# First sequence of an attention and channel-mix kernel by halves of its heads, with its second scores turned round, a ScalarE share in the weight conversion, and gates begun with the first heads

## The chip, the cores and the metric

One core of a Trainium2 chip. The metric is device time in microseconds for one execution, the median of three runs. Engines are named as in the profile: PE is TensorE, DVE is VectorE, ACT is ScalarE, POOL is GpSimd, SP is SyncE, which here only issues loads and stores.

## The reference

```python
B, H, S, D = 8, 8, 576, 64;  NP = 32;  DM, DF = 512, 1024
def sm_attn(qq, kk, vv):
    s = scale * qq @ kk.T;  a = exp(s - max(s))
    return (a / (sum(a) + 1e-9)) @ vv
packed = sm_attn(p, k, v)            # 32 packed rows a head
out    = sm_attn(q, packed, packed)  # 576 tokens a head
x  = out, heads side by side         # (8, 576, 512)
xp = x, shifted by one token
xk = mu_k * x + (1 - mu_k) * xp;  xr = mu_r * x + (1 - mu_r) * xp
return sigmoid(xr @ w_r) * (relu(xk @ w_k) ** 2 @ w_v)
```

The activations are fp32, the three weight matrices arrive as 64-bit floats.

## The kernel before

The 4608 tokens are cut into nine blocks of 512. For every block PE multiplies gates (`w_r`, 48 products), keys (`w_k`, 96) and values (`w_v`, 96); each product is 512 columns wide. An fp32 product is three products of fp32r parts, high by high, high by low and low by high. This makes 2160 wide products (`gates`, L976 to L978; `keys`, L936 to L938; values, L1005 to L1007).

The weights are converted on the chip: `convert` takes a piece of 128x512, makes an fp32 pattern out of the two 32-bit halves of each number (ACT L309, DVE L311, L313, L315) and splits it into high (ACT L319) and low (DVE L321). There are 20 pieces: `w_r` 4, `w_k` 8, `w_v` 8.

The attention of a sequence has these steps: keys and queries are loaded (`raw`) and transposed on PE against `ident` (L415, queries of the first sequence L455); p is made block-diagonal with a stream transpose (`pt`, L482); first scores (L503); maximum, exponential (L585, L592); the softmax weights transposed (L606, L607); their product with the values (L532); the packed rows transposed (L553); second scores with the packed rows on partitions (L667 for the first sequence, L687 for others); a stream transpose on DVE, the softmax over 32 entries, and a stream transpose back (L703 and on). For later sequences x is then multiplied (L746) and mixed with its shifted copy on ACT and DVE (L897, L901). For the first one the shares mu and 1-mu are multiplied into the packed rows (`shared`, L783, L791), and PE makes xr and xk of the first block right out of the softmax weights `a2t` (`mixed_on_pe`, L806), by halves of the tokens (`hf`).

The order of the work is not written by hand. `Flow` runs all these parts as generators; each step names its engine and an estimated time, and the planner takes the step that can start first, ties and near ones by a rank (`RANK_...`, `FIRST`). The result is one fixed list for each engine. Where it sees PE waiting, ahead of `keep_busy`, it writes fill products (`spare`, L1085), 128x128 against `ident`, whose result nobody reads. `gates` of the first block ends that time. All loads are issued by `load` (L227), on SP's queue. In the time of the first loads the planner has ACT and DVE shared between attention and conversion.

Of the kernel before, what the change touches and what calls it, by code (L numbers as in the profile page):

```python
# [182 lines left out]
def attn_pack_channel_mix(ctx: ExitStack, tc: tile.TileContext, q, k, v, p, mu_k, mu_r, w_k, w_v, w_r, out):  # L183
    nc = tc.nc
# [21 lines left out]
    FIRST = 9.944, 10.165, 11.85, 12.0  # L206
    RANK_1, RANK_MIX, RANK_KEYS, RANK_R, RANK_W, RANK_W2, RANK_V, LOADS_1, RANK_SQ, RANK_REST, HOLD_V, HOLD_S = 12.793, 9.086, 9.325, 12.0, 13.15, 14.582, 15.08, 14.446, 12.17, 12.101, 0.1, 0.1
# [17 lines left out]
    def load(dst, src, issue, us):  # L225
        yield "queue", issue, None, None
        nc.sync.dma_start(dst, src)  # L227
        begin = max(flow.free.get("dma", 0.0), flow.t + 0.46)
        flow.free["dma"] = begin + us
        flow.free["queue"] = max(flow.free["queue"], begin - 2.0)  # L230
        flow.now.t = begin + us + LANDS
# [58 lines left out]

    def convert(w, hi, lo, c, o, n, event, first=None):
# [15 lines left out]

        yield act(n)
        nc.scalar.activation(m.bitcast(F32), w1.bitcast(F32), AF.Copy, scale=2.0 ** -112)  # L309
        yield vec2(n)  # L310
        nc.vector.tensor_scalar(m, m, 3, None, op0=ALU.logical_shift_left)  # L311
        yield vec(n, after=0.0)
        nc.vector.scalar_tensor_tensor(m, w1, 0x80000000, m, op0=ALU.bitwise_and, op1=ALU.bitwise_or)  # L313
        yield vec(n, after=0.0)
        nc.vector.scalar_tensor_tensor(m, w0, 29, m, op0=ALU.logical_shift_right, op1=ALU.bitwise_or)  # L315
# [17 lines left out]

    def loads(b):
        flow.spawn(packed(b), lrank(b) - (0.03 if b else 0.015))
        for src, tag in ((k, "kT"), (v, "vt"), (q, "qT")):
# [5 lines left out]
            if b == 0 and tag == "qT":  # L342
                yield from first_queries()
                continue
            for pr in range(NPR):

                space = "xk" if b == 0 else "raw"
# [24 lines left out]
    def back_to_issue():  # L372
        flow.now.t = flow.free["queue"]

    def values_of(b, h):

        slot = yield from flow.take("vt")
        vt = tile_([P, NPR, 5 * D], F32, "vt", slot)
        if b < MOVED:
            yield from load(  # L380
                vt[:, :, :4 * D], v[b, h::2, :NQ, :].rearrange("h (p c) d -> p h (c d)", c=4), 0.46, 1.8
            )
            back_to_issue()
            yield from load(vt[:S - NQ, :, 4 * D:], v[b, h::2, NQ:, :].rearrange("h p d -> p h d"), 0.63, 0.45)
# [20 lines left out]
    def transposed_on_pe(tag, b, pr, raw_space, raw_slot, raw):  # L405
# [11 lines left out]
        yield act(S)  # L417
        nc.scalar.copy(t.rearrange("p (a b) -> p a b", a=2), pT[:, :, :HS])
# [3 lines left out]

    def first_queries():

        raws = []
        for pr in range(NPR):
            space = "xk" if pr == NPR - 1 else "raw"
            slot = yield from flow.take(space)
            raws.append((space, slot, tile_([P, 6, 2 * D], F32, space, slot, "raw")))
        for pr, (space, slot, raw) in enumerate(raws):  # L430
            for hh in range(2):
                yield from load(
                    raw[:T6, :, hh * D:(hh + 1) * D], q[0, 2 * pr + hh].rearrange("(c p) d -> p c d", p=T6), 0.51, 0.6,
                )
                back_to_issue()
            for hf in range(2):
                flow.spawn(
                    first_transposed(pr, hf, space, slot, raw), rank(0) + (0.02 if hf else 0.0), flow.free["dma"] + LANDS
                )

    def first_transposed(pr, hf, raw_space, raw_slot, raw):
# [16 lines left out]
        if pr % 2:  # L458
# [8 lines left out]
    def packed(b):  # L467
# [16 lines left out]
        flow.set(("pt", b))  # L484

# [8 lines left out]
    def front(b):  # L494
# [23 lines left out]
        together = b > 0  # L518
        if together:
            yield from flow.wait(*((tag, b, h) for tag in ("aT", "vt") for h in range(2)))  # L520
            yield pe(1.4)
        for h in range(2):
            if not together:
                yield from flow.wait(("aT", b, h), ("vt", b, h))
                yield pe(0.65)
# [33 lines left out]
        first = None  # L559
        if b == 0:  # L560
            sx = yield from flow.take("xt")

            a2 = tile_([P, 2, S + 1], F32, "xt", sx, "a2t")
            nc.gpsimd.memset(a2[:, :, 0:1], 0.0)
            first = dict(a2=(sx, a2), left=4)
            flow.spawn(shared(ppT, first), RANK_MIX - 0.1)
            for hf in range(2):
                flow.spawn(half_scores(hf, sp, pm, ppT, left, first), rank(b, hf) - 1)
            return
# [89 lines left out]
    def half_scores(hf, sp, pm, ppT, left, first):  # L659

        yield from flow.wait(*(("qT", 0, pr, hf) for pr in range(NPR)))
        slot = yield from flow.take("pa")
        yield pe(0.7)
        s2 = banks(slot)
        for pr in range(NPR):
            for h, own in enumerate(HALVES):
                nc.tensor.matmul(  # L667
                    s2[32 * pr:32 * pr + 32, h, :HS], ppT[own, 32 * pr:32 * pr + 32],
                    ts["qT", 0, pr][1][own, hf * HS:(hf + 1) * HS],
                    start=True, stop=True,  # L670
                )
        flow.set(("s2", 0, hf))
        if ("s2", 0, 1 - hf) in flow.when:
            for pr in range(NPR):
                flow.give("kq", ts.pop(("qT", 0, pr))[0])
        yield from back(0, hf, sp, pm, slot, s2, left, first)

    def scores(b, sp, pm, ppT, left):
# [16 lines left out]
        for hf in range(2):  # L695
            flow.spawn(back(b, hf, sp, pm, slots[hf], s2[hf], left, None), rank(b, hf) - 1)

    def back(b, hf, sp, pm, slot, s2, left, first):
# [8 lines left out]
        m2 = sb.tile([P, NTB], F32, name="m2", tag=f"m2{hf}")  # L707
# [15 lines left out]
        if first:  # L723
            yield vec(S)
            nc.vector.transpose(
                first["a2"][1][:, :, 1 + hf * HS:1 + (hf + 1) * HS].rearrange("p h (k b) -> p h k b", b=32),
                e.rearrange("p (h k) b -> p h k b", h=2),
            )
            flow.give("e", se)
            for j, res, tag in ((2, xrs, "xr"), (0, xks, "xk")):  # L730
                flow.spawn(mixed_on_pe(hf, j, res, tag, first), RANK_MIX if tag == "xr" else RANK_KEYS)
            if hf:
                flow.spawn(rest_of_first(sp, pm, first), RANK_REST)
            return
# [42 lines left out]
    def shared(ppT, first):  # L777

        yield from flow.wait("mu")
        st = yield from flow.take("sig")  # L780
        ppTs = tile_([P, 4, NPR, NP], F32, "sig", st, "ppTs")
        yield vec(4 * P)
        nc.vector.tensor_tensor(  # L783
# [330 lines left out]
```

## Time and profile before

| | us |
|---|---|
| median of three runs | 597.06 (596.43 to 598.03) |
| profiled execution, its span from first to last instruction | 594.0 |
| PE busy in it | 584.2 |
| DVE / ACT busy | 370.9 / 309.2 |
| first gate product / first key product begins | 37.67 / 57.53 |

The profiled execution shows its span alone; the 3.06 us to the median are what lies around it and the spread. A busy PE counts fill products too. An instruction of fp32 operands leaves two records on PE, so that 24 records of `spare` are 12 instructions. Starts of successive records are a better measure of a product than its duration, since records overlap.

### The profile page before, as it was taken

To read this page: it belongs to the slowest core of one execution; us is meant where nothing else is said; L and a number is where in the kernel's file an instruction comes from. 1 tells how busy PE (TensorE), PEld (TensorE's weight loads), DVE (VectorE), ACT (ScalarE), POOL (GpSimd) and SP (SyncE) were. 2 spreads that over 40 slices of the span, in tenths; PEclk is the share of its full clock that TensorE was granted. 3 is DMA by queue.
4 is the path that set the end of the run, shared out by engine and by line. 5 is a ranking of instruction groups with operands and counts; after the bars stand their busy time and mean duration, and the time that the engine had idled before them with its cause. 6 is when DMAs were issued, how large, how long until landed. Compare 5 with 4: busy or idle time off the path is not lost.

```text
span 594.0 us, 10276 instructions
## 1 busy us (share of the span) xinstructions
PE 584.2 (98%) x3965; PEld 458.9 (77%) x3965; DVE 370.9 (62%) x721; ACT 309.2 (52%) x548; POOL 2.1 (0%) x22
## 2 busy tenths in 40 slices
PE   9999999999999999999999999999999999999997
PEld 8776767787778777777777787777788888888885
DVE  2698999956692788867874698269314712641321
ACT  3557884644663458468537392548425613721410
POOL 0000000000000000000000000000000000000000
PEclk9999999999999999999999999999999999999999
DMA  8988460764727076486076375200100010001001
GB/s 214 266 207 258 164 139 17 162 173 73 150 46 189 12 154 143 129 143 141 3 195 135 65 140 134 58 1 1 72 1 1 1 72 0 1 0 72 0 1 71
DMA packets 164095, 56.51 MB, mean 95 GB/s; under 512 B 141000, under 2 KB 155344, under 8 KB 164048
## 3 DMA queue, kind: packets, MB, share of 16 engines
q1 hardware_dynamic: 164048, 55.87, 39.3%
q8 instruction: 31, 0.51, 0.4%
q14 instruction: 16, 0.13, 0.1%
HBM read 42.86 MB, written 12.98 MB: 94 GB/s over the span
## 4 chain that ended last, share of the span: by engine, by line
PE 80%; DVE 13%; SPq 3%; DMA 1%; issue 1%; ACT 1%; DVEq 0%
PE ph L936 10%; PE pvo L1005 10%; PE ph L937 10%; PE ph L938 10%; PE pvo L1007 10%; PE pvo L1006 10%; PE pr L976 5%; PE pr L977 5%; PE pr L978 5%; SPq L227 3%; DVE m L313 2%; DVE m L315 2%; PE pa L532 2%; PE pa L746 2%; PE pa L687 1%
## 5 line engine op out<-in xcount | busy, mean ns | idle before, releaser
L936 PE MATMUL ph<-xk,wk_h 128*128 128x512 f32 x288 | 114.8, 399 | 0.0
L1005 PE MATMUL pvo<-wv_h,sq 128*128 128x512 f32 x288 | 113.8, 395 | 0.0
L937 PE MATMUL ph<-xk,wk_h 128*128 128x512 f32 x288 | 112.5, 391 | 0.0
L938 PE MATMUL ph<-xk,wk_l 128*128 128x512 f32 x288 | 112.3, 390 | 0.0
L1006 PE MATMUL pvo<-wv_l,sq 128*128 128x512 f32 x288 | 112.2, 389 | 0.0
L1007 PE MATMUL pvo<-wv_h,sq 128*128 128x512 f32 x288 | 112.1, 389 | 0.0
L954 DVE CAST sq<-r 128x512 fp32r<-128x512 f32 x72 | 30.0, 416 | 122.0 <-ACT r L950 119.4
L947 ACT ACTIVATE r<-ph 128x512 f32<-128x512 f32 x72 | 43.0, 597 | 85.8 <-PE ph L938 85.5
L1005 PEld LDWEIGHTS pvo<-wv_h,sq 128*128 128x128 f32 x288 | 54.0, 188 | 16.5 <-issue 5.4
L936 PEld LDWEIGHTS ph<-xk,wk_h 128*128 128x128 f32 x288 | 54.1, 188 | 16.0 <-issue 4.1
L1007 PEld LDWEIGHTS pvo<-wv_h,sq 128*128 128x128 f32 x288 | 54.1, 188 | 11.4
L938 PEld LDWEIGHTS ph<-xk,wk_l 128*128 128x128 f32 x288 | 54.1, 188 | 11.4
L937 PEld LDWEIGHTS ph<-xk,wk_h 128*128 128x128 f32 x288 | 54.1, 188 | 11.0 <-DVE xk L843 0.6
L1006 PEld LDWEIGHTS pvo<-wv_l,sq 128*128 128x128 f32 x288 | 54.1, 188 | 10.7
L976 PE MATMUL pr<-wr_h,xr 128*128 128x512 f32 x144 | 57.5, 399 | 0.4 <-DVE sig L1016 0.3
L901 DVE SCALAR_TENSOR_TENSOR x<-xt,mus,x 128x64 f32<-128x64 f32 (+7 forms) x120 | 54.0, 495 | 6.0 <-ACT x L897 5.9
L977 PE MATMUL pr<-wr_l,xr 128*128 128x512 f32 x144 | 56.2, 390 | 0.0
L978 PE MATMUL pr<-wr_h,xr 128*128 128x512 f32 x144 | 56.1, 390 | 0.0
L897 ACT ACTIVATE x<-xt,mus 128x64 f32<-128x64 f32 (+7 forms) x120 | 54.4, 514 | 0.1
L987 ACT ACTIVATE sig<-pr 128x512 f32<-128x512 f32 x36 | 21.4, 601 | 60.7 <-PE pr L978 47.4
L956 DVE TENSOR_TENSOR sq<-r,sq 128x512 fp32r<-128x512 f32 x72 | 49.4, 686 | 1.4
L1016 DVE TENSOR_TENSOR sig<-pvo,sig 128x512 f32<-128x512 f32 x36 | 24.0, 687 | 39.0 <-PE pvo L1007 39.0
(102 smaller groups left out, 693.6 us busy)
## 6 DMA issues: line engine op xcount, KB each, us to landing
out<-sig SPq DMA_DIRECT2D x36, 256.0 KB, 2.6
raw<-in_k SPq DMA_DIRECT2D x96, 72.0 KB, 2.7
raw<-in_q SPq DMA_DIRECT2D x96, 72.0 KB, 2.8
st<-in_moe_w_k SPq DMA_DIRECT2D x8, 512.0 KB, 5.2
st<-in_moe_w_v SPq DMA_DIRECT2D x8, 512.0 KB, 4.7
vt<-in_v SPq DMA_DIRECT2D x24, 160.0 KB, 3.4
away<-blocks SPq DMA_DIRECT2D x12, 288.0 KB, 2.7
vt<-in_v SPq DMA_DIRECT2D x24, 128.0 KB, 3.8
```

The lines of the kernel that those rows point to most:

```text
L897: nc.scalar.mul(x32[:, o:o + n], xts[b, c][:, 1 + s:1 + s + n], mus[:, j, c:c + 1])
L901: nc.vector.scalar_tensor_tensor(x32[:, o:o + n], xts[b, c][:, s:s + n], mus[:, j + 1, c:c + 1], x32[:, o:o + n], op0=ALU.mult, op1=ALU.add,)
L936: nc.tensor.matmul(ph, wk_h[:, c, fs], xh, start=(c == 0), stop=False)
L937: nc.tensor.matmul(ph, wk_h[:, c, fs], xl, start=False, stop=False)
L938: nc.tensor.matmul(ph, wk_l[:, c, fs], xh, start=False, stop=(c == NC - 1))
L956: nc.vector.tensor_tensor(hl[:, 1, :], r, hl[:, 0, :].bitcast(F32), op=ALU.subtract)
L976: nc.tensor.matmul(pr, xh[:, ts_], wr_h[:, c, :], start=(c == 0), stop=False)
L977: nc.tensor.matmul(pr, xh[:, ts_], wr_l[:, c, :], start=False, stop=False)
L978: nc.tensor.matmul(pr, xl[:, ts_], wr_h[:, c, :], start=False, stop=(c == NC - 1))
L1005: nc.tensor.matmul(pv[t], sh, wv_h[:, f, :], start=(f == 0), stop=False)
L1006: nc.tensor.matmul(pv[t], sh, wv_l[:, f, :], start=False, stop=False)
L1007: nc.tensor.matmul(pv[t], sl, wv_h[:, f, :], start=False, stop=(f == NF - 1))
```

## The change

- The first sequence runs by halves of its heads (`first_side(h)`, four heads each): keys, queries and values of heads 0 to 3 are loaded first. First scores of a half are four products of 64 rows and 64 columns (L555); the value product goes into another bank (L576), and what doesn't belong to a head is masked while it is scaled (L589).
- Second scores have tokens on partitions (L610): for each of five chunks of 128 tokens and two pairs of heads the queries are the stationary operand. The softmax works on 128x640 (L623 to L636), and PE transposes it back (L643), with ACT copies (L648, L650), in place of two stream transposes on DVE.
- The mix (`mixed_on_pe`, L956) is four products of 512 columns and 64 rows for each half and each of xr, xk; before, sixteen of 32 rows and 64 columns for each half of the tokens. The shares come as rows repeated over 64 partitions, by eight loads on POOL's queue (`first_constants`); DVE makes 1-mu (L687) and multiplies with the packed rows (L695). `shared` with its four transposes goes.
- `first_gates` starts with channels 0 and 1, which are heads 0 to 3, for three of the four token tiles (L1112 to L1114), then channels 2 and 3, then the last tile.
- `convert`: ACT's operation carries the sign (Prelu, L331), so that DVE's L313 goes in all 20 pieces; in the first 8 ACT also brings the low bits into place (L329), so that L311 goes there too.
- p and the shares' rows are loaded by ACT's queue; ranks and holds are new numbers.

```diff
-        nc.scalar.activation(m, w1, AF.Copy, scale=2.0 ** -112)
-        nc.vector.tensor_scalar(m, m, 3, None, op0=ALU.logical_shift_left)
-        nc.vector.scalar_tensor_tensor(m, w1, 0x80000000, m, op0=ALU.bitwise_and, op1=ALU.bitwise_or)
-        nc.vector.scalar_tensor_tensor(m, w0, 29, m, op0=ALU.logical_shift_right, op1=ALU.bitwise_or)
+        by_act = len(pieces_split) < RANK_LATE13
+        if by_act:
+            nc.scalar.activation(w0, w0, AF.Copy, scale=2.0 ** -29 * (1 - 2.0 ** -22), bias=-0.5)
+        nc.scalar.activation(m, w1, AF.Prelu, scale=2.0 ** -112, alpha=2.0 ** 32)
+        if by_act:
+            nc.vector.scalar_tensor_tensor(m, m, 3, w0, op0=ALU.logical_shift_left, op1=ALU.bitwise_or)
+        else:
+            nc.vector.tensor_scalar(m, m, 3, None, op0=ALU.logical_shift_left)
+            nc.vector.scalar_tensor_tensor(m, w0, 29, m, op0=ALU.logical_shift_right, op1=ALU.bitwise_or)
...
+    def first_side(h):
+        j0, own = 2 * h, slice(h * P, (h + 1) * P)
...
+                nc.tensor.matmul(
+                    s1[half, hf, :HS], pts[0][1][:, j0 + j, :], ts["kT", 0, j0 + j][1][:, hf * HS:(hf + 1) * HS],
...
+        for k, (at, _) in enumerate(CHUNKS):
+            for j in range(2):
+                nc.tensor.matmul(
+                    s2[:, k * P + 64 * j:k * P + 64 * j + 64], ts["qT", 0, j0 + j][1][:, at:at + P],
+                    ppT[:, 64 * j:64 * j + 64], start=True, stop=True,
...
+            nc.tensor.transpose(back_[:, bank, col:col + rows], e[:rows, k], ident[:rows, :rows])
...
+    def first_constants():
+        for h in range(2):
+            for j, mu in ((2, mu_r), (0, mu_k)):
+                for c in range(2):
+                    at = (2 * h + c) * P
+                    yield from load(
+                        t[64 * c:64 * c + 64, j], mu[at:at + P].unsqueeze(0).broadcast_to([64, P]), 1.0, 0.02, "gpsimd"
...
-        first_products(px, n, a2, [
-            (1 + hf * HS - t, lambda own, h, t=t: shares_of[own, j + t, h * D:(h + 1) * D]) for t in range(2)
+        for t in range(2):
+            for c, half in enumerate(HALVES):
+                nc.tensor.matmul(
+                    px[:, c, :TB], shares_of[half, j + t, :], a2[half, h, 1 - t:1 - t + TB], start=(t == 0), stop=(t == 1),
...
+        for part, (cs, tiles) in enumerate(((range(2), range(3)), (range(2, 4), range(3)), (range(4), range(3, 4)))):
```

The planner's list for PE ahead of the first gate product stood so in before (line, operation, tile<-operands, shape and count of instructions; `spare` is fill, L415 the second sequence's key transposes):

```order
L667 MATMUL pa<-qT,ppT 32x288 x8
L455 MATMUL pq<-ident,raw 128x96 x6
L1085 MATMUL spare<-ident 128x128 x5
L667 MATMUL pa<-qT,ppT 32x288 x8
L1085 MATMUL spare<-ident 128x128 x20
L415 MATMUL pa<-ident,raw 128x96 x6
L1085 MATMUL spare<-ident 128x128 x2
L415 MATMUL pa<-ident,raw 128x96 x6
L1085 MATMUL spare<-ident 128x128 x5
L806 MATMUL pa<-a2t,pms 64x288 x16
L1085 MATMUL spare<-ident 128x128 x7
L976 MATMUL pr<-wr_h,xr 128x512
```

In the changed kernel the same stretch, from the second half's second scores on (L610; those of the first half stand ahead of it, with the second half's values and twelve query transposes between), reads:

```order
L610 MATMUL pa<-both,qT 128x64 x10
L1248 MATMUL spare<-ident 128x128
L643 MATMUL pa<-ident,e 128x112 x4
L643 MATMUL pa<-ident,e 128x128
L1248 MATMUL spare<-ident 128x128 x5
L462 MATMUL pa<-ident,raw 128x96 x6
L956 MATMUL pa<-a2t,mub 128x512 x4
L462 MATMUL pa<-ident,raw 128x96 x6
L1248 MATMUL spare<-ident 128x128 x4
L462 MATMUL pa<-ident,raw 128x96 x6
L1248 MATMUL spare<-ident 128x128
L1112 MATMUL pr<-wr_h,xr 128x512
```

From the last scores to the first gate product stand 11 fill products in place of 34, and the first mix (L956) stands ahead of the second half's transposes back (L643), which follow right behind the first gate products.

On DVE the first instructions of before were these (the conversion of one piece of `w_r`, then p, then the first maximum):

```order
L311 TENSOR_SCALAR m<-m 128x512
L313 SCALAR_TENSOR_TENSOR m<-st,m 128x512
L315 SCALAR_TENSOR_TENSOR m<-st,m 128x512
L321 TENSOR_TENSOR wr_l<-m,wr_h 128x512
L482 STREAM_TRANSPOSE pt<-pin 128x128
L585 TENSOR_REDUCE mx<-pa 128x1 x2
L587 TENSOR_SCALAR nmx<-mx 128x1 x2
```

And in the changed kernel these (`mub` are the loaded shares of a half, L781 the maximum of a half):

```order
L1220 COPY mus<-pu 128x2x4
L1222 TENSOR_SCALAR mus<-pu 128x2x4
L541 STREAM_TRANSPOSE pt<-pin 128x256
L687 TENSOR_SCALAR mub<-mub 128x2x128
L781 TENSOR_REDUCE mx<-pa 128x1
L783 TENSOR_SCALAR nmx<-mx 128x1
L687 TENSOR_SCALAR mub<-mub 128x2x128
L781 TENSOR_REDUCE mx<-pa 128x1
```

No piece is converted ahead of the first scores any more, and L687, which waits for loads on POOL's queue, stands in front of either half's maximum.

## Rows read from the trace of the kernel before

**Rows 1.** Head of the page: span, and busy time by engine
```profile
span 594.0 us, 10276 instructions
...
PE 584.2 (98%) x3965; PEld 458.9 (77%) x3965; DVE 370.9 (62%) x721; ACT 309.2 (52%) x548; POOL 2.1 (0%) x22
```

**Rows 2.** Busy time by stage; start and end first, then length and engines
```profile
0.00:25.00 25.00, 22.36 (x270) 19.50 (x271) 9.17 (x22) 10.56 (x21) 0.80 (x9) 1.00 0.87 233
25.00:57.50 32.50, 30.52 (x297) 23.20 (x296) 30.03 (x61) 20.21 (x40) 0.00 (x0) 1.00 0.85 234
57.50:100.00 42.50, 41.42 (x345) 30.24 (x344) 41.82 (x85) 31.21 (x60) 0.10 (x1) 1.00 0.46 127
...
116.30:590.00 473.70, 473.38 (x2950) 374.20 (x2950) 272.64 (x523) 235.00 (x402) 1.02 (x10) 1.00 0.33 73
```

**Rows 3.** Timeline of PE to 20 us: start, duration, line, tile, records
```profile
1.41 5.79 PE L1085 MATMUL spare<-ident 128*128 128x128 f32 x26 [1.41 <-POOL ident masks.py:199]
7.04 0.66 PE L415 MATMUL pa<-ident,raw 96*128 96x96 f32 x6
7.53 0.64 PE L1085 MATMUL spare<-ident 128*128 128x128 f32 x4
...
11.46 1.20 PE L503 MATMUL pa<-kT,pt 64*32 64x288 f32 x32
12.59 2.94 PE L1085 MATMUL spare<-ident 128*128 128x128 f32 x24
15.37 0.64 PE L606 MATMUL pa<-ident,a 128*128 128x128 f32 x4
...
17.89 0.90 PE L532 MATMUL pa<-vt,aT 128*32 128x64 f32 x40
18.72 0.47 PE L455 MATMUL pq<-ident,raw 96*128 96x96 f32 x3
```

**Rows 4.** Timeline of PE, from the fills behind the second scores to the first key
```profile
27.40 4.73 PE L1085 MATMUL spare<-ident 128*128 128x128 f32 x40
...
34.67 1.48 PE L806 MATMUL pa<-a2t,pms 32*64 32x288 f32 x32
36.08 1.83 PE L1085 MATMUL spare<-ident 128*128 128x128 f32 x14
37.67 0.47 PE L976 MATMUL pr<-wr_h,xr 128*128 128x512 f32 x1
...
44.30 0.39 PE L976 MATMUL pr<-wr_h,xr 128*128 128x512 f32 x1
...
46.12 0.39 PE L978 MATMUL pr<-wr_h,xr 128*128 128x512 f32 x1
...
57.53 0.39 PE L936 MATMUL ph<-xk,wk_h 128*128 128x512 f32 x1
```

**Rows 5.** Timeline of PE behind the first key product
```profile
60.00 1.53 PE L503 MATMUL pa<-kT,pt 64*32 64x288 f32 x32
```

**Rows 6.** Groups by line on DVE: busy us, mean ns, idle before
```profile
L313 DVE SCALAR_TENSOR_TENSOR m<-st,m 128x512 uint32<-128x512 uint32 x20 | 13.7, 687 | 0.4
...
L585 DVE TENSOR_REDUCE mx<-pa 128x1 f32<-128x576 f32 x16 | 11.5, 742 | 5.9 <-PE pa L503 5.9
...
L311 DVE TENSOR_SCALAR m<-m 128x512 uint32<-128x512 uint32 x20 | 8.3, 415 | 5.3 <-ACT m L309 5.3
```

**Rows 7.** Group of the conversion's first operation on ScalarE
```profile
L309 ACT ACTIVATE m<-st 128x512 f32<-128x512 f32 x20 | 13.4, 686 | 6.1 <-DMA st<-in_moe_w_r 2.7 <-DMA st<-in_moe_w_v 1.8 <-DMA st<-in_moe_w_k 1.4
```

**Rows 8.** Timeline of SP's issues: start, time in issuing, line, count
```profile
6.16 1.93 SPq L227 DMA_DIRECT2D pin<-in_p  x4
...
10.69 7.44 SPq L227 DMA_DIRECT2D raw<-in_q  x8
```

**Rows 9.** Loads issued before 30 us: KB each, median us to landing
```profile
raw<-in_k SPq DMA_DIRECT2D x12, 144.0 KB, 3.5
...
st<-in_moe_w_k SPq DMA_DIRECT2D x2, 512.0 KB, 8.5
```

More of the change, by code (lines that the diff above doesn't have):

```diff
@@ L486, in two_slots, with first_others, first_shares @@
+    def first_others(h, t):
+        yield from reached()
+        yield vec(2 * P)
+        nc.vector.tensor_scalar(t[:, 1::2], t[:, 0::2], -1.0, 1.0, op0=ALU.mult, op1=ALU.add)
+        firsts["shares", h] = t
+        flow.set(("mub", h))
+    def first_shares(h, pm):
+        yield from flow.wait(("mub", h))
+        t = firsts["shares", h]
+        yield vec(4 * P)
+        nc.vector.tensor_tensor(t, t, pm.unsqueeze(1).broadcast_to([P, 4, P]), op=ALU.mult)
+        flow.set(("pms", h))
     def two_slots():
@@ L517, in front @@
         pv = banks(slot)
[L518 to L521, printed above, removed]
+        yield from flow.wait(*((tag, b, h) for tag in ("aT", "vt") for h in range(2)))
+        yield pe(1.4)
         for h in range(2):
-            if not together:
-                yield from flow.wait(("aT", b, h), ("vt", b, h))
-                yield pe(0.65)
             sv, vt = vts.pop((b, h))
@@ L657, in weights_moved @@
         flow.set(("aT", b, h))
[L659 to L676, printed above, removed]
     def scores(b, sp, pm, ppT, left):
@@ L801, in first_products, with mixed_on_pe @@
-    def first_products(px, n, a2, terms):
-        for term, (at, weights) in enumerate(terms):
-            for pr in range(NPR):
-                own = slice(32 * pr, 32 * pr + 32)
-                for h, half in enumerate(HALVES):
-                    nc.tensor.matmul(
-                        px[pr // 2][half, pr % 2, :n], weights(own, h), a2[own, h, at:at + n],
-                        start=(term == 0), stop=(term == len(terms) - 1),
-                    )
-    def mixed_on_pe(hf, j, res, tag, first):
-        a2 = first["a2"][1]
-        yield from flow.wait("pms")
+    def mixed_on_pe(h, j, res, tag):
+        a2 = firsts["a2"][1]
+        yield from flow.wait(("pms", h))
@@ new lines, in mixed_on_pe @@
+        flow.set(("mixed", h, tag))
+        multiplied = flow.t
+        for c in range(2):
+            sx = yield from flow.take(space)
+            hl = tile_([P, 2, TB], F32R, space, sx, tag)
+            xh, xl = hl[:, 0, :], hl[:, 1, :]
+            x = px[:, c, :TB]
+            yield act(TB, after=multiplied)
+            nc.scalar.copy(xh, x)
+            yield vec(TB)
+            nc.vector.tensor_tensor(xl, x, xh.bitcast(F32), op=ALU.subtract)
+            if c:
+                flow.give("pa", slot)
+            res[0, 2 * h + c] = sx, xh, xl
+            flow.set((tag, 0, 2 * h + c))
@@ new lines, in rest_of_first @@
+    def rest_of_first():
+        n = S - TB
+        yield from flow.wait(*(("mixed", h, tag) for h in range(2) for tag in ("xr", "xk")))
+        sx, a2 = firsts["a2"]
+        slot = yield from flow.take("pa")
+        yield pe(0.7)
+        px = banks(slot)
+        for h in range(2):
+            for c, half in enumerate(HALVES):
+                nc.tensor.matmul(
+                    px[:, c, h * P:h * P + n + 1], firsts["pm", h][1][half], a2[half, h, TB:], start=True, stop=True,
+                )
+        for h in range(2):
+            flow.give("pm", firsts["pm", h][0])
+            flow.give("sig", firsts["mu", h])
+        flow.give("sig", firsts["both"])
```

387 lines of the change are left out of this document (254 added, 133 removed).

## Prediction, made before the changed kernel ran

> **What bounds the kernel now.** I read the page's head first: TensorE (PE) is busy 584.2 of 594.0 us [rows 1], so the time can only fall if PE does less, or idles less. The table by stages tells where [rows 2]: from 116.3 us to 590 PE is busy 473.38 of 473.70, and from 57.5 to 100 it is busy 41.42 of 42.50. Behind 57.5 nothing is left to win. Before it PE is busy 22.36 of 25.00 and 30.52 of 32.50, which looks nearly as full; but the timeline shows that much of this "busy" is the fill matmul `spare` [rows 3, 4], which computes nothing. It stands where the planner saw PE waiting: 26 records from 1.41 on, and 24, 40 and 14 records at 12.59, 27.40 and 36.08, and smaller groups between, 78 matmuls (156 records) in all. So the start is a chain of latencies with fill laid into its gaps, and its end is the first key product, at 57.53. Behind that PE runs 2160 wide products without a gap, 0.2275 us apart (eight of them from 44.30 to 46.12 are 1.82) [rows 4]. **The time is the moment of the first key plus a fixed amount of work.** VectorE (DVE) is the second thing to watch: 30.03 of 32.50 busy from 25 us on, and 41.82 of 42.50 from 57.5 on [rows 2]; it converts weights there.
>
> **The ledger of before, up to the first key.** PE executes in the order written, so I add the groups in that order, each from the start of its first record to the start of the next group's. First fills end at 7.04. Key transposes: 8 of 0.49 (7.04 to 7.53) = 3.9. Fills after the first: 65 matmuls of two records; the 24 records at 12.59 lasted to 15.37, so 0.23 a matmul = 15.0. First scores: 11.46 to 12.59 = 1.13. Transposes of the softmax weights: four records and a short fifth at 15.37, 0.6; twice = 1.2. Values: 17.89 to 18.72 = 0.83, twice = 1.7. Query transposes: half as many records, 8 of half the 0.49 = 2.0. Second scores: twice 16 records where the first scores had 32 in 1.13, with their edges two of 0.85 = 1.7. Small transposes 0.9. Token mix on PE: four of 1.41 (34.67 to 36.08) = 5.6 [rows 4]. Gates: 48 of 0.2275 = 10.9. Some ten switches between kinds of work, 0.1 each = 1.0. Sum 52.0; the measured 57.53 leaves 5.5, of which 3.2 is idle time (57.5 less 22.36 and 30.52 is 4.6, and 1.41 of it is the very start) and 2.3 is not assigned.
>
> **The change, by the same ledger.** The order after has 37 fills instead of 78: 8 at the start, 29 later.
> Start: I put the first fill at 1.5 (one more clearing stands ahead on POOL); 16 records at (7.04-1.41)/26 = 0.2165 end at 5.0. Later fills 29 x 0.23 = 6.7. Key transposes of both sequences 3.9, query transposes 2.0, as before.
> First scores by halves: 4 products a half with 64 rows and 64 columns, two row halves side by side. Before, 32 records of 288 columns in eight places at once took 1.13, i.e. four rounds; the new ones are eight records in two places, four rounds again: 1.13 a half, 2.3.
> Transposes of weights 1.2, values 1.7, small transposes 0.5.
> Second scores, tokens on partitions: 20 records a half, each 64 columns against 128 stationary ones. The trace has no such product. Below: 64 columns at the pace of 288 in 0.24 are 0.055 each, 1.1 a half; above: a fill record, 128 against 128, 0.115, 2.3 a half. The weight load changes at every record as it does for the fills, so I take 2.0, twice = 4.0.
> Transposes back, on PE now instead of on DVE: 0.6 a half, 1.2.
> Mix: 4 products of 512 columns, 8 records in two row halves. If halves overlap as in the first scores, four rounds of 512/288 x 0.24 = 0.43, with an edge 1.95; four of them 7.8. If they don't, 8 x 0.43 = 3.4 and 0.2, and all four cost 6.8 more.
> Gates 10.9 (the same 48). Now ahead of the first key stand also the rest of the first sequence (4 products of 65 columns, an estimated 0.4) and the second sequence's first scores, 1.4; in before both came behind it, the latter at 60.00 [rows 5], so they are moved, not added (with their switches 1.95). Switches 1.0.
> Sum 50.0. To this come waits: in before the records up to 7.04 came at 0.2165, the later fills at 0.116, so what now stands from 5.0 to 7.0, key transposes, may run at the slow pace as well, 0.9; the last transposes back wait for their softmax 0.5; first mixed rows and weights at the gates 0.6; 1.0 for all that before's unassigned 2.3 stands for. 3.0, against 5.5 in before, since 41 fills fewer means a chain that PE has less time to wait out. **First key at 53.0**, which has to be held against 57.53 + 1.95 = 59.5: **gain 6.5**.
>
> **Do other engines allow it?** (1) DVE loses one operation in all 20 pieces, 0.687 each, and one in the first 8, 0.415 each [rows 6]: 13.7 + 3.3 = 17.0. Most of it lies in the stage where DVE is full. ScalarE pays 8 x 0.69 = 5.5 [rows 7] for the low bits; the sign costs nothing there if the other function (Prelu) takes what the copy of this shape took, 0.686; no row shows Prelu, and I put its bounds a tenth to either side. ScalarE is busy 20.21 of 32.50 and 31.21 of 42.50 [rows 2], so that has room. (2) The half softmax: five operations on 640 columns, by the maximum's 0.742 for 576 [rows 6] 0.82 each, 4.4 us with its small ones, from second scores to transposes back. For the first half PE has between these two the other half's values (0.85), twelve query transposes (1.0), six fills (1.4) and the other half's scores (2.0), 5.3: hidden with some 0.6 to spare. For the second half it has, by the order shown, the first half's transposes back, eleven fills, three key transposes, a mix and a gate, 7.2; on DVE four operations of the conversion (0.69 each) are laid into the same chain, 7.2 as well: that is the wait of 0.5 counted. (3) SP issues keys, then half the queries, then values. An issue costs it 0.48 (four `pin` in 1.93) to 0.93 (eight query loads in 7.44) [rows 8]. The loads of p and of the shares' rows, which stood between, are now on ScalarE's queue, ahead of its first copy. The first three pieces of w_r come behind 20 loads of keys, queries and values, issued from about 10.5 to 19; with the 8.5 that the slowest weight piece of this stretch took to land [rows 9] the last is there at 19 to 27.5, and a conversion (five operations, 3.4) ends at 31 at worst, 1 us behind the first gate but needed one gate group later. I count nothing for it beyond the 0.6.
>
> **The new wait.** The shares come by eight loads on POOL's queue. DVE has to wait for four of them in front of its first maximum and for the other four in front of the second (order above): behind this instruction stand the maxima, the exponentials and all that follows, on every engine. No row has a load issued by POOL. Low bound: SP's 0.48 an issue; begun at about 2.5 and landed 3.5 later, as the key loads, the last is there at 9.9, before the second maximum (about 13.4): hidden. High bound: 0.93 an issue and the 8.5 of the slowest landing, 18.4, 5.0 late, and the end moves by that. I take it as hidden, since these loads are of 32 KB and the row nearest in size is `pin`, and keep the 5.0 for the range (592 to 595.5). The Trainium skill, page "SBUF — State Buffer", section "Who interferes with whom", says that descriptors for such loads are not written while VectorE runs an operation in a two-port mode, and the page gives some 620 ns alone against 3100 ns overlapped. By the larger figure, an estimate, eight loads would be there at about 27, 14 us late, and the run would be at 604. No run here shows it yet; in the order after, DVE has only three short operations ahead of that wait, which speaks against it.
>
> **Rivals.** A: the waits go away as well (PE's chain is short enough that the 3.0 is 1.0, and second scores cost 1.1 a half): gain 10, 586.5 to 587. For it: 41 fills fewer. Against: the trace's gaps never closed so far. B: the row halves of the mix don't run side by side: gain 6.5 - 6.8, about none, 597. Against it: L503's 1.13, which can only be with several at once. C: gates begin early but xk, the key weights or the second sequence's scores come late, so PE idles behind the first key; the gain is given back by what is late. DVE at 41.82 of 42.50 speaks for it, the 17.0 taken from it against. 3 to 5 us, 593.5 to 595.5. D, the slower side: POOL's loads. They decide from the point at which the last four land later than 13.4 + 6.5 + 1.8 = 21.7, that is (21.7 - 2.5 - 3.5)/8 = 2.0 us an issue, four times SP's; each further us costs one. At 2.4 an issue they land at 25.2 and the time is 602.
>
> **The numbers.** The span of 594.0 lies 3.06 below the median of the runs, 597.06; I take this distance as kept: span 587.5, **590.5**. 0.3%, 1.8 us, is about what a measurement here can tell from no change (595.3 to 598.9). Chances: the forecast, 588 to 593.5: 0.66. A, below 588: 0.12. C, or loads 3 to 5 late, 593.5 to 595.3: 0.07. B, or C that takes all: 0.09. D: 0.06. Faster 0.85, same 0.09, slower 0.06. Range: 586.0 to 595.0 leaves out the same and slower cases and some of A.
>
> **What would show it.** First gate at about 30 (37.67 in before), first key at 53, PE 473 us from there less 1.95. Second scores 2.0 a half, mix 1.95, first scores 1.13. No row of DVE that waits for `mub` before the first or second maximum by more than 1 us. DVE's busy time down by some 15 in the stretch to 100. It is wrong if the mix rows take 3.4, if DVE stands waiting for POOL's loads, or if PE shows gaps of over 2 us between gates and keys.

## The result, and the profile after

The changed kernel takes 590.22 us (589.84 to 591.14, four runs); the kernel before, with one more run beside these, 597.37. The ratio is 0.9885, 95% interval 0.9871 to 0.9899: faster by 1.15%. 590.5 was forecast, in a range of 586.0 to 595.0.

The page's head, to be held against [rows 1]:

```profile
span 588.6 us, 9896 instructions
...
PE 580.0 (99%) x3778; PEld 455.0 (77%) x3778; DVE 354.5 (60%) x683; ACT 313.5 (53%) x556; POOL 7.3 (1%) x36
```

The profiled execution is 5.4 us shorter than that of before, the medians lie 7.15 apart. The difference is in the execution that was profiled before: every run of the changed kernel lists its span, and its time lies 1.82 to 1.84 above it (590.42 and 588.6), so by the same distance the profiled 594.0 was a run of about 595.8, one of the quicker ones of before. (Two executions of before with spans of 594.0, timed beside the experiments, took 595.75 and 595.78.)

The quicker and the longer executions of before differ in TensorE's granted clock. Of the 51 timed beside the experiments, 27 have a mean granted clock of 0.999 or 1.000 and a median of 595.35, and 24 have 0.990 to 0.997 and a median of 597.88. The profiled one has 1.000, and all four executions of the changed kernel have 0.999 or 1.000. So at an equal clock the gain is about 5, and some 2 of the 7.15 go with executions of before that lost clock. No trace of such an execution was kept, so where it lost the clock is not shown. One execution of experiment 3, 727.40 us at a mean granted clock of 0.754, is left out of every comparison.

The table by stages (start and end, then length, busy time of PE, PE's weight loads, DVE, ACT and POOL, granted clock, DMA), cut at the moment forecast for the first key:

```profile
0.00:25.00 25.00, 23.18 (x244) 20.37 (x244) 9.94 (x25) 11.43 (x27) 6.01 (x23) 1.00 0.92 234
25.00:53.00 28.00, 26.14 (x174) 16.89 (x173) 21.59 (x37) 23.37 (x46) 0.11 (x1) 1.00 0.89 271
53.00:57.50 4.50, 4.50 (x22) 3.70 (x21) 4.02 (x10) 4.49 (x9) 0.00 (x0) 1.00 0.79 289
57.50:100.00 42.50, 41.46 (x322) 31.46 (x321) 37.95 (x78) 36.45 (x72) 0.10 (x1) 1.00 0.53 132
...
116.30:584.60 468.30, 468.15 (x2930) 370.23 (x2928) 266.29 (x510) 232.21 (x397) 1.02 (x10) 1.00 0.32 72
```

Against [rows 2]: DVE has 37.95 of 42.50 from 57.5 on where it had 41.82, and ACT 36.45 where it had 31.21. PE's idle time there is the same as before (1.04, before 1.08). PE's share of "busy" at the start is again high, with less fill in it: 74 records of `spare` against 156.

The timeline of PE, the places that the ledger named:

```profile
1.59 3.79 PE L1248 MATMUL spare<-ident 128*128 128x128 f32 x16 [1.59 <-POOL ident masks.py:199]
...
9.21 1.19 PE L555 MATMUL pa<-kT,pt 128*64 128x288 f32 x8
10.33 0.71 PE L462 MATMUL pa<-ident,raw 96*128 96x96 f32 x6
...
17.58 2.34 PE L610 MATMUL pa<-both,qT 128*128 128x64 f32 x20
19.85 0.90 PE L576 MATMUL pv<-vt,aT 128*32 128x64 f32 x40
...
25.90 0.66 PE L643 MATMUL pa<-ident,e 112*128 112x112 f32 x5
...
28.42 1.99 PE L956 MATMUL pa<-a2t,mub 64*128 64x512 f32 x8
30.34 0.72 PE L462 MATMUL pa<-ident,raw 96*128 96x96 f32 x6
...
32.56 0.48 PE L1112 MATMUL pr<-wr_h,xr 128*128 128x512 f32 x1
...
35.07 0.71 PE L643 MATMUL pa<-ident,e 112*128 112x112 f32 x5 [1.55 <-DVE xr L969]
...
40.87 0.50 PE L1112 MATMUL pr<-wr_h,xr 128*128 128x512 f32 x1
41.21 0.39 PE L1113 MATMUL pr<-wr_l,xr 128*128 128x512 f32 x1
...
42.02 1.99 PE L956 MATMUL pa<-a2t,mub 64*128 64x512 f32 x8 [0.18 <-ACT kT L474]
...
55.40 0.39 PE L1068 MATMUL ph<-xk,wk_h 128*128 128x512 f32 x1
...
60.96 0.72 PE L462 MATMUL pa<-ident,raw 96*128 96x96 f32 x6 [0.65 <-ACT a L788]
...
63.22 0.75 PE L802 MATMUL pa<-ident,a 128*128 128x128 f32 x4 [0.32 <-ACT qT L474]
```

First scores of a half 9.21 to 10.33 = 1.12, second scores 17.58 to 19.85 = 2.27, transposes back 25.90 to 26.40 = 0.50, mix 28.42 to 30.34 = 1.92. The first gate product is at 32.56 (37.67 in before), the first key product at 55.40 (57.53, with 1.95 of moved work 59.5). Behind the first three gate products PE stands 1.55 us and is released by DVE; at 60.96 and 63.22 it stands 0.65 and 0.32 for the second sequence.

What DVE and ACT did at these places:

```profile
7.61 0.29 DVE L687 TENSOR_SCALAR mub<-mub 128x256 f32<-128x256 f32 x1 [0.66 <-DMA mub<-in_moe_mu_k]
10.44 0.76 DVE L781 TENSOR_REDUCE mx<-pa 128x1 f32<-128x576 f32 x1 [2.54 <-PE pa L555]
...
11.42 0.29 DVE L687 TENSOR_SCALAR mub<-mub 128x256 f32<-128x256 f32 x1
14.78 0.76 DVE L781 TENSOR_REDUCE mx<-pa 128x1 f32<-128x576 f32 x1 [3.07 <-PE pa L555]
...
34.32 0.69 DVE L969 TENSOR_TENSOR xr<-pa,xr 128x512 fp32r<-128x512 f32 x1 [1.36 <-ACT xr L967]
```

```profile
33.17 0.65 ACT L329 ACTIVATE st<-st 128x512 uint32<-128x512 uint32 x1 [1.38 <-DMA st<-in_moe_w_r]
33.72 0.57 ACT L967 CAST xr<-pa 128x512 fp32r<-128x512 f32 x1
...
58.78 1.28 ACT L788 ACT_TABLE_LOAD   x1
60.08 0.74 ACT L788 ACTIVATE a<-pa,nmx 128x576 f32<-128x576 f32 x1
```

The waits for `mub`: 0.66 us at 7.61, none at 11.42, both far ahead of the maxima. The wait of PE at 35.07 goes back through DVE's split of xr at 34.32 (idle 1.36) to ACT's copy of xr at 33.72, and that stood behind ACT's conversion at 33.17, which had waited 1.38 for a piece of w_r. At the other place ACT begins the second sequence's exponentials at 60.08, behind conversions, sigmoids and a table load at 58.78.

The loads on POOL's queue (start, time in issuing, count):

```profile
1.67 0.66 POOL L242 DMA_DIRECT2D mub<-in_moe_mu_r  x1
...
2.99 0.52 POOL L242 DMA_DIRECT2D mub<-in_moe_mu_r  x1
3.50 1.03 POOL L242 DMA_DIRECT2D mub<-in_moe_mu_k  x2
4.51 1.05 POOL L242 DMA_DIRECT2D mub<-in_moe_mu_r  x2
5.52 1.06 POOL L242 DMA_DIRECT2D mub<-in_moe_mu_k  x2
```

An issue takes 0.52 to 0.66, and all eight are out by 6.6.

### The profile page after: what moved, and what is told of

It is laid out like the page before. It is cut to its first block, busy times and chain, and to the rows that moved or that the text cites. A ratio compares the mean times of both kernels' runs of the same rounds, so it can differ in the third digit from the quotient of the medians.

```text
span 588.6 us, 9896 instructions
## 1 busy us (share of the span) xinstructions
PE 580.0 (99%) x3778; PEld 455.0 (77%) x3778; DVE 354.5 (60%) x683; ACT 313.5 (53%) x556; POOL 7.3 (1%) x36
## 4 chain that ended last, share of the span: by engine, by line
PE 90%; ACT 5%; DMA 2%; DVE 1%; issue 1%; SPq 0%; POOL 0%; ACTq 0%; DVEq 0%; POOLq 0%
PE pvo L1163 11%; PE ph L1068 11%; PE pvo L1164 11%; PE pvo L1165 11%; PE ph L1069 11%; PE ph L1070 11%; PE pr L1134 5%; PE pr L1135 5%; PE pr L1136 5%; PE pa L911 2%; PE pa L739 2%; PE spare L1248 1%; PE pa L864 1%; PE pa L715 1%; DMA st<-in_moe_w_r 1%
## 5 line engine op out<-in xcount | busy, mean ns | idle before, releaser
L1029 ACT ACTIVATE x<-xt,mus 128x192 f32<-128x192 f32 (+7 forms) x120 | 55.7, 515 | 1.1 <-DVE xr L1051 1.1
L1134 PE MATMUL pr<-wr_h,xr 128*128 128x512 f32 x128 | 50.6, 396 | 0.0
L1135 PE MATMUL pr<-wr_l,xr 128*128 128x512 f32 x128 | 49.9, 390 | 0.0
L1136 PE MATMUL pr<-wr_h,xr 128*128 128x512 f32 x128 | 49.8, 389 | 0.0
L1082 ACT ACTIVATE r<-r 128x512 f32<-128x512 f32 x72 | 45.4, 633 | 1.7
```

Source lines behind the costliest of these rows:

```text
L1029: nc.scalar.mul(x32[:, o:o + n], xts[b, c][:, 1 + s:1 + s + n], mus[:, j, c:c + 1])
L1134: nc.tensor.matmul(pr, xh[:, ts_], wr_h[:, c, :], start=(c == 0), stop=False)
L1135: nc.tensor.matmul(pr, xh[:, ts_], wr_l[:, c, :], start=False, stop=False)
L1136: nc.tensor.matmul(pr, xl[:, ts_], wr_h[:, c, :], start=False, stop=(c == NC - 1))
```

## The experiments

Each was timed in rounds beside the kernel before; its time is compared with the changed kernel's 590.22, which was measured in other rounds, so that differences of less than 1 us between two of these times are uncertain. Where "the same order" is said, all other instructions of every engine stand as in the changed kernel; "planned anew" means that `Flow` has laid all work out again with the same constants, so that such a run shows the edit and a new order together.

**1. Work in front of the first key.** Same order.

```diff
+                if (i, f, c) == (0, 0, 0):
+                    for _ in range(10):
+                        nc.tensor.matmul(ph, wk_h[:, c, fs], xh, start=True, stop=True)
                 nc.tensor.matmul(ph, wk_h[:, c, fs], xh, start=(c == 0), stop=False)
```

> Changed kernel with ten more products of 512 columns right in front of the first key product (their result is overwritten by the real one); nothing else moves. Theory: the time is the moment of the first key product plus fixed work, so 10 x 0.2275 = 2.3 us more than the changed kernel's 590.2: 592.5. Rival, there is slack behind the first key: less than 0.8 more, 590.2 to 591.0.

590.38 (589.75 to 591.02): nothing. The theory fell. The timeline of PE:

```profile
54.79 2.43 PE L1070 MATMUL ph<-xk,wk_h 128*128 128x512 f32 x10
57.05 0.39 PE L1071 MATMUL ph<-xk,wk_h 128*128 128x512 f32 x1
...
61.82 0.66 PE L462 MATMUL pa<-ident,raw 96*128 96x96 f32 x6
...
63.53 0.67 PE L802 MATMUL pa<-ident,a 128*128 128x128 f32 x4
```

The real first key product is at 57.05, 1.65 later than in the changed kernel (this execution was 0.61 ahead at the ten products, 54.79 against 55.40), but the second sequence's transposes at 61.82 and 63.53 no longer wait: 0.86 later than there, then 0.31, and the last product of the run ends 0.2 later. What holds PE there is the chain of the second sequence, not the number of products ahead of it.

**2. Work in front of the first gate.** Same order; ten products likewise, in `first_gates`.

> Changed kernel with ten more products of 512 columns right in front of the first gate product, 2.3 us of work. Theory A, the start is a sum of PE's work: 2.3 more, 592.5. Theory B, the start is a chain of latencies through ScalarE and VectorE: behind the first gate product PE stood still for 1.55 us (VectorE's split of xr was late), so 1.55 of the 2.3 are free and the time is 0.7 more, 591.0.

590.23 (589.85 to 590.72). 2.3 us of added work show as 0.6 at the second half's transposes back and at the second mix, 0.3 at the third mix, and nothing behind 61 us. So B, and below its own number, since PE's wait for the second sequence took the rest.

**3. Fill twice, 4. fill left out.** Same order; this is 3, and in 4 the new line is `if flow.fills <= 8:`.

```diff
 def fill():
-    nc.tensor.matmul(spare[:, :P], ident, ident, start=True, stop=True)
+    flow.fills = getattr(flow, "fills", 0) + 1
+    for _ in range(1 + (flow.fills > 8)):
+        nc.tensor.matmul(spare[:, :P], ident, ident, start=True, stop=True)
```

> Changed kernel with each of its 29 later fill products written twice, 29 x 0.23 = 6.7 us more of work that computes nothing. Theory A, sum of PE's work: 6.7 more, 597. Theory B, chain of latencies: PE's own idle time ahead of the first key is only 2.1 us behind the start, 1.55 of it in one place, so 1.6 to 2.1 are swallowed and 4.6 to 5.1 remain, 595.

> Changed kernel with the first 8 fill products alone, the 29 later ones left out. Theory A, sum of PE's work: 6.7 less, 583.5. Theory B, chain of latencies with fill in its gaps: idle time takes the place of the fill, 589.5 to 591. Rival C, the fill keeps TensorE's pace up: transposes and scores run at the slow pace of the first records (0.2165 in place of 0.116) and 3 us or more are added, 593 or above.

Twice the fill: 593.66 (593.38 to 594.07), 3.4 more for 6.7 of work. None behind the first 8: 589.36 (588.86 to 589.56), 0.9 less for 6.7 of work. Both lie on B's side: 1.3 below its number for 3, and just under its range for 4. The 0.9 fits a small loss from fill that stands in front of work that is ready. Without it the gates' start reads:

```profile
31.52 0.47 PE L1112 MATMUL pr<-wr_h,xr 128*128 128x512 f32 x1
...
33.89 0.71 PE L643 MATMUL pa<-ident,e 112*128 112x112 f32 x5 [0.84 <-DVE xr L969]
```

1.04 earlier than in the changed kernel for the first gate, 1.18 for the transposes back; in this execution the granted clock stayed at 1.00 in every 5 us up to 45. The other four have a mean of 0.997 over the run, against 0.999 or 1.000 in the changed kernel.

**5. VectorE's relief from the sign taken back.** Same order; one more operation in each of 20 pieces that sets a bit already set, behind the last of the steps that make the pattern.

```diff
+        nc.vector.scalar_tensor_tensor(m, w1, 0x80000000, m, op0=ALU.bitwise_and, op1=ALU.bitwise_or)
         flow.give("sq", slot)
```

> Changed kernel with VectorE setting the sign bit once more in each of the 20 pieces, at the place where the kernel before did it: 20 x 0.69 = 13.7 us of VectorE work that changes nothing in the result; every other instruction stands as in the changed kernel. Theory: the relief of VectorE is a part of the gain, since three of these operations stand in the second half's softmax and in front of xr, and VectorE is 37.95 of 42.50 busy from 57.5 to 100 us: first gates 1 to 2 us later, end 1.0 to 2.5 later, 591.2 to 592.7. Rival: VectorE is nowhere on the path, 589.9 to 590.6.

601.85 (601.53 to 605.27), ratio to before 1.0091 (1.0062 to 1.0119): 11.6 us for 13.7 of VectorE work, far above what I expected, and slower than the kernel before. The table by stages:

```profile
25.00:53.00 28.00, 23.23 (x135) 14.74 (x134) 24.06 (x40) 20.68 (x40) 0.12 (x1) 1.00 0.78 245
...
57.50:100.00 42.50, 36.99 (x296) 27.16 (x296) 38.30 (x76) 31.61 (x59) 0.00 (x0) 0.96 0.50 131
```

Three shorter stages of the same trace:

```profile
63.00:66.00 3.00, 1.06 (x5) 0.56 (x3) 2.90 (x6) 1.71 (x2) 0.00 (x0) 1.00 1.00 279
...
75.00:80.00 5.00, 2.85 (x59) 2.15 (x52) 4.90 (x13) 3.51 (x7) 0.00 (x0) 0.92 1.01 265
80.00:85.00 5.00, 5.00 (x44) 2.76 (x44) 4.93 (x11) 2.27 (x5) 0.00 (x0) 0.74 0.80 183
```

PE is busy 23.23 of 28.00 where it was 26.14, and 36.99 of 42.50 where it was 41.46, while VectorE is at 24.06 and 38.30. The first key product comes 3.7 later and the rest of the 11.1 in spans is lost between 55 and 108 us. PE's two longest waits there fall where VectorE is full: 3.04 us at 67.09 for an exponential of ScalarE, which had itself waited 1.98 at 64.28 for an added operation, and 2.15 at 79.46 for VectorE directly. From 57.5 to 100 the granted clock is 0.96: it fell to 0.74 from 80 to 85 us, behind a stretch in which PE was busy 2.85 of 5. So a part of the price is the pace of TensorE after idling; by what is missing to 1.00 in these two rows it is 1.7 us, an estimate. The order is fixed here, so 11.6 is the price in this order and not in one made for the added work.

**6. The new conversion alone**, in the kernel before, with that kernel's constants (planned anew).

> Kernel before with the new weight conversion alone (sign by ScalarE in 20 pieces, low bits by ScalarE in 8); the planner's constants are those of before. Theory: the gain is in the first sequence's shorter chain, so the conversion alone moves the time by less than 1 us, 596 to 598 in runs whose before is 597. Rival: the conversion is the source of the gain, 593 or less.

595.51 against 596.89 of before on that chip, ratio 0.9976 (0.9957 to 0.9994): 1.4 us, less than a quarter of the gain. Among executions with a mean granted clock of 0.999 or 1.000 alone it is 0.8 (594.76 against 595.6). The profiled execution of this run, at 0.993, shows where it lost clock: 0.50 from 20 to 25 us, behind 2.5 us (from 15.0 on) in which PE was busy 1.20.

**7. The old conversion in the changed kernel**, planned anew.

> Changed kernel with the weight conversion of before (sign and low bits on VectorE in all 20 pieces), planned anew. Theory, after the run with the sign bit set again: ScalarE and VectorE set the pace from 25 to 108 us once the front is short, so most of the gain goes without the relief: 595 to 600. Rival: the planner lays the 17 us of VectorE work where it waits, as in the kernel before, and the gain is kept: 590 to 592.

610.65 (608.71 to 611.1), ratio 1.0236 (1.0206 to 1.0266), worse than either theory. One row of the waits between 25 and 110 us (waiting engine, line, releaser; total, times, longest) has most of it:

```profile
PE pa L455 <- ACT a L781: 13.4, 1, 13.4
```

The first gate is at 32.99, as in the changed kernel. But in the new order the second sequence's transposes, scores and values stand between the first block's gates, and PE waits 13.40 us there for one exponential. From 50 to 75 us VectorE is busy 24.52 of 25.00 and ScalarE 16.60, and from 60 to 75 us the granted clock is 0.50, so the work behind the wait is slow as well. With old conversion and these constants the order is a bad one; what the old conversion would cost in an order made for it is left open.

**8. Gates of the first block in the common order** (a token tile takes all four channels before the next begins), planned anew; `first_gates` isn't called.

> Changed kernel with the first block's gates in the common order (a token tile takes all four channels before the next begins), planned anew. Theory: twelve products, 2.7 us, which the changed kernel does between the first half's and the second half's mix, have to come behind the second mix; of this the wait at 61 to 63 us for the second sequence's weights, 1.35, hides a part: 1.4 to 2.7 later, 591.6 to 592.9. Rival: the order of gates doesn't matter, since the second half's chain sets the end of both, 589.7 to 590.7.

591.72 (590.54 to 592.54): 1.5 more, with a range that overlaps the changed kernel's (589.84 to 591.14). Rows of PE, first gate and first key product:

```profile
34.06 0.48 PE L1134 MATMUL pr<-wr_h,xr 128*128 128x512 f32 x1
...
58.52 0.39 PE L1068 MATMUL ph<-xk,wk_h 128*128 128x512 f32 x1
```

The first key is 3.1 later than in the changed kernel, and a part of that doesn't reach the end, as in 1.

**9. POOL's loads made late.** Same order; each of the eight loads is cut into four of 32 columns.

```diff
                     yield from load(
-                        t[64 * c:64 * c + 64, j], mu[at:at + P].unsqueeze(0).broadcast_to([64, P]), 1.0, 0.02, "gpsimd"
+                        t[64 * c:64 * c + 64, j, :32], mu[at:at + 32].unsqueeze(0).broadcast_to([64, 32]), 1.0, 0.02, "gpsimd"
                     )
+                    for o in range(32, P, 32):
+                        nc.gpsimd.dma_start(
+                            t[64 * c:64 * c + 64, j, o:o + 32], mu[at + o:at + o + 32].unsqueeze(0).broadcast_to([64, 32])
+                        )
```

> Changed kernel with each of the eight loads on POOL's queue cut into four of 32 columns, 32 issues in place of 8; nothing else moves. At 0.52 us an issue from 1.67 on and 3.5 to landing, the first half's shares are there at 13.5 (its maximum was taken at 10.44) and the second half's at 22 (14.78). Theory: such a wait holds both halves' chains, and the end moves by most of the 7 us: 594 to 597. Rival: the queue's loads are far off the path and the fills give way, less than 2 us, 590 to 592.

606.73 (606.14 to 609.62), 16.5 more, above the expected. Rows of DVE, the two operations that wait for `mub`, and four stages between 10 and 40 us:

```profile
15.32 0.32 DVE L691 TENSOR_SCALAR mub<-mub 128x256 f32<-128x256 f32 x1 [8.06 <-DMA mub<-in_moe_mu_r]
...
27.14 0.29 DVE L691 TENSOR_SCALAR mub<-mub 128x256 f32<-128x256 f32 x1 [10.65 <-DMA mub<-in_moe_mu_k]
```

```profile
10.00:15.00 5.00, 2.19 (x20) 1.69 (x19) 0.00 (x0) 0.64 (x1) 3.25 (x7) 1.00 1.09 296
15.00:20.00 5.00, 2.59 (x12) 2.02 (x14) 1.14 (x3) 3.00 (x8) 4.12 (x9) 0.62 1.02 206
...
25.00:30.00 5.00, 1.10 (x5) 1.11 (x6) 2.26 (x7) 1.10 (x3) 0.00 (x0) 0.64 0.28 60
...
35.00:40.00 5.00, 5.00 (x61) 4.43 (x61) 3.55 (x7) 2.75 (x8) 0.00 (x0) 0.50 0.11 25
```

The last load was there at 27.1, where DVE starts on it, not at 22: an issue took 0.51 to 0.65, as before, but from the eighteenth on POOL also waited for earlier loads. DVE stood 8.06 and 10.65 us and the second maximum was 12.6 late. PE idled meanwhile (2.19 of 5.00 busy, then 1.10 of 5.00), and its granted clock went to 0.62 and 0.50 (0.50 is the lower of its two levels, 1.2 GHz; in this trace a value between is a stretch with both), so that the transposes and scores that followed came later still: the second half's second scores begin 17.0 later than in the changed kernel, at 40.46 instead of 23.44.

**10. Low bits back on VectorE, sign still on ScalarE**, planned anew (ScalarE brings the low bits into place in none of the pieces).

> Changed kernel with ScalarE carrying the sign in all pieces, but the low bits on VectorE in all (before: the first 8 pieces on ScalarE), planned anew. VectorE gets 8 x 0.415 = 3.3 us, ScalarE loses 8 x 0.68 = 5.5. Theory: VectorE's time is what counts, at the 11.1 for 13.7 of the run with the sign bit set again: 2.7 later, 592 to 594. Rival: ScalarE, 4.49 of 4.50 busy at 53 to 57.5, is what holds the second sequence's exponentials: 588.5 to 589.8.

589.63 (589.04 to 590.09), 0.6 less: 3.3 us more of VectorE's work cost nothing in an order made for it. The rival's side, though not to be told from the changed kernel with certainty. The first key is at 53.59, 1.8 earlier, and VectorE is full later on:

```profile
70.00:85.00 15.00, 15.00 (x101) 11.41 (x104) 14.93 (x31) 10.67 (x19) 0.00 (x0) 1.00 0.40 96
```

**11. A piece of w_r earlier, without late fill**, planned anew.

> Changed kernel without its 29 later fill products, and with the fourth piece of w_r loaded ahead of the second sequence's p and keys, planned anew. Theory: the piece that landed at 33.14 held ScalarE by 1.4 and so PE at 33.5 to 35; with it earlier, the second half's transposes back come 1 us or more earlier, and the end 0.5 to 1.5 below the run without fill (589.4): 588 to 589. Rival: the second sequence, whose loads now come later, or VectorE holds the end: 589.2 or more.

590.54 (590.17 to 590.74). Two rows of the table by stages:

```profile
8.00:11.00 3.00, 1.38 (x13) 0.87 (x11) 1.20 (x3) 1.37 (x3) 0.00 (x0) 1.00 1.12 262
...
14.00:17.00 3.00, 3.00 (x15) 1.61 (x13) 0.00 (x0) 1.15 (x4) 0.00 (x0) 0.50 1.08 237
```

PE was busy 1.38 of 3.00 from 8 us on, and behind that its granted clock is 0.50: this order leaves PE idle where fill would have stood. So the run doesn't answer what the late piece costs; a version with the piece early and the fill kept was not run.

**12. 10 with the 15 last fills left out**, same order as in 10.

> The run with the low bits on VectorE in all pieces (589.63), with its last 15 fill products left out (those behind the first half's second scores) and the 21 earlier ones kept, every other instruction in the same order. Theory: fill in the queue delays the work behind it, as in the run without the 29 later products (0.9 below the changed kernel, first gate 1.0 earlier), and the earlier fill is enough to keep TensorE's granted clock at 1.00: 588.6 to 589.3. Rival: the late fill stood where PE would have waited anyway, or what it gave is lost at the second sequence: 589.4 to 590.

589.67 (589.14 to 591.27): nothing gained over 10. The first gate came 0.7 earlier and the first key 0.2 later. This is the rival.

The best time of all is 4's, 589.36: 0.9 below the changed kernel, and its five runs lie below all four of that, and below all twelve of 1 and 2, which were timed in the same rounds (lowest 589.75).

## Why the prediction was right, and where it was not

- **The terms of PE's ledger held.** First scores 1.12 (1.13 forecast), mix 1.92 (1.95, so the row halves do run side by side, and rival B is out), transposes back 0.50 (0.6), the 16 slow fill records from 1.59 on, with the next work at 5.31 (1.5 and 5.0). Second scores took 2.27 where 2.0 was taken; 2.3 had been the upper end. PE's longest gap between gates and keys is 1.55, under the 2 that would have spoken against the forecast.
- **The first key came 2.4 late, and all of it was lost behind the first gate.** "First gate at about 30" left the waits out: the terms that stand ahead of it add up to about 30 alone and to about 32.5 with the waits 0.9, 0.6 and 1.0, and it came at 32.56. From there to the first key the sum has some 20.4, the trace 22.84. The wait at 35.07 is 1.05 of the difference (1.55 where 0.5 stood), that at 42.02 is 0.18, and most of the rest is switches between kinds of work: the first gate product behind other work takes 0.34 (40.87 to 41.21) where 0.2275 is the pace. At 35.07 it is not the softmax that was late: the sum priced VectorE's chain for that place, and the trace shows ScalarE standing until 33.17 for a w_r piece that SP had issued at 27.37. Of the loads I had followed only the first three pieces; the fourth stands behind the second sequence's keys on SP's queue.
- **Two errors of the other sign.** Up to the first key the gain is 59.5 - 55.4 = 4.1, not 6.5. Behind it the changed kernel is 1.3 shorter by spans (594.0 - 57.53 - 1.95 = 534.5, and 588.6 - 55.4 = 533.2), which I had put at nothing; together these are the 5.4. And the 3.06 between span and median that I took as kept is 1.82 in the runs of the changed kernel; the other 1.2 is that the execution profiled before was quicker than the median one. The forecast was 594.0 - 6.5 + 3.06, the profiled run is 594.0 - 5.4 + 1.82: that they agree to 0.1 is luck, since 1.1 too much gain and 1.2 too much distance cancel; that the gain in spans came within 1.1 is not.
- **"Behind 57.5 nothing is left to win" was wrong by a little, and the picture behind it by more.** Experiment 1 put 2.3 us in front of the first key and found 0.2 in the end: the second sequence's chain sets PE's place at 61 to 64 us. Adding PE's work gave a good number, but a microsecond of it isn't worth a microsecond (0.07, 0 and 0.5 per us in 1, 2 and 3; 0.13 in 4). Two readings of before were off without entering the sum: 473 us is what PE has from 116.3 us on, not from the first key on, and 48 of the 2160 wide products stand ahead of that key.
- **VectorE's 17 us were priced at nothing, and the forecast rests on them.** The text named them as what speaks against rival C and left it there. Experiment 5 prices the sign's 13.7 of them in the changed kernel's own order: 0.85 us for each us, the fall of the clock included. The 3.3 of the low bits could go back at no cost once the order was made anew (experiment 10). Experiment 6 shows that in the kernel before, with its longer start, the conversion alone brings 1.4. So in these orders the gain is neither part's own: with the short start and without the relief VectorE sets the pace, full at PE's longest waits in 5 and at the long one in 7. Whether an order made for the old conversion could keep the short start's gain is open. What I should have done is to price the short start without the relief.
- **"DVE's busy time down by some 15 in the stretch to 100" failed.** It fell by 7.5 (81.02 to 73.50 by the rows of the two tables). Over the whole run it fell by 16.4, near the 17.0 reckoned, so more than half of the fall shows behind 100 us and not where DVE was full.
- **Rival D was rightly put aside, with a wrong price.** An issue of POOL took 0.52 to 0.66 (0.48 had been the low bound), 3.4 to 3.7 to landing, and neither maximum waited for `mub`; the one wait for it, 0.66, ended 2.8 us ahead of the first. VectorE ran for only some 0.3 of the 1.06 us in which the last two were issued, and they were no longer than the others. By the Trainium skill, page "SBUF — State Buffer", section "Who interferes with whom", a VectorE operation in a two-port mode holds up the descriptors of such loads while it runs; no run here shows that rule at work, and none speaks against it. "Each further us costs one" is wrong: the second maximum came 12.6 late in experiment 9 and the run took 16.5 more, with the clock down after PE had idled.
- **Begun gates are worth about 1.5** (experiment 8, planned anew, with overlapping ranges), less than the 3.1 by which they move the first key.
- What part of the gain each remaining piece of the change has (halves of heads, turned scores, the mix in four products) was not taken apart.

## What to carry to other kernels

Price the cover as well as the gain: where an edit shortens a chain on one engine, ask what the next engine would do without the other edits of the same change, and let a run put the removed work back in the unchanged order (an operation that changes nothing, close to the old place). The price found so holds for that order alone. Before a sum of work is trusted as "the time", add a known amount in front of the supposed bound; two microseconds that vanish show that the bound is elsewhere. And compare runs with runs: a profile is one execution, and here the two profiles differ by 1.7 us less than the medians. The mean granted clock of each run is worth reading beside its time.

## What the hardware did that I had not expected

- TensorE's granted clock fell to half (0.50) in 14 to 17 us of experiment 11 after PE had been busy 1.38 of 3 us (and 1.71 of the next 3, at 0.61), and to 0.62 and 0.50 in experiment 9 after 2.19 of 5 and 1.10 of 5. In experiment 4's profiled execution it stayed at 1.00 without the same fill; the mean of the other four is 0.997. Whether fill can be left out depends, in these runs, on the order that remains, and 0.9 us was the most that came of it.
- The kernel before lost some of its clock in 24 of 51 executions (mean 0.990 to 0.997, 2.5 us in the medians), the changed kernel in none of four and its variants of experiments 1 and 2 in none of twelve.
- POOL's queue took an issue in 0.52 to 0.66 us, within the 0.48 to 0.93 of SP's [rows 8], and in experiment 9 it waited for earlier loads to land from the eighteenth of 32 on (0.68, 0.23, 0.82 and 0.85 us).
- Prelu took the place of the copy on ScalarE at no cost: 0.685 us a piece in the mean of 20 (the copy 0.686 in [rows 7]).
